# A GEGLU kernel on one core: the order of its first loads (gate rows on two queues ahead of the second block of x, the kept gate blocks in one stretch, then three transposing transfers)

## Chip, cores, metric

The kernel runs on one NeuronCore of one Trainium2 chip. The metric is the device time of one execution in microseconds (us), lower is better.

## The reference

```python
# x: 32 x 32 x 1024 (1024 tokens), w_gate, w_up: 1024 x 3584, w_down: 3584 x 1024, all bf16
def reference(x, w_gate, w_up, w_down):
    return (gelu(x @ w_gate) * (x @ w_up)) @ w_down      # tanh form of gelu
```

## The kernel before

The kernel multiplies by a one-level Strassen scheme: each matrix is cut into four quarters and some products are made on sums of quarters. TensorE (PE) runs almost without a pause. The first work it gets is a set of products "ahead": 24 column tiles of the lower rows of `w_gate` (the kept blocks `a12a` and `a12b`, numbers 0 to 5, four tiles each) times one quarter of the transposed x (`b21`). They need little data, so they fill the time in which the rest of x and the weights arrive.

The head, cut to what matters here (SyncE and ScalarE each issue to a DMA queue, q1 and q10 on the page; `KD` is 4 blocks of 128 rows, `KQ` is 2):

```python
load_nat(nc.sync, 0, 0, HALF)              # first block of x, not transposed: half on each queue
load_nat(nc.scalar, 0, HALF, NB_P)
...
load_ahead(0, 0, 1)                        # first gate rows, 128 KB, SyncE
load_nat(nc.scalar, 1, 0, NB_P)            # second block of x, 128 KB in packets of 256 B, ScalarE
load_ahead(0, 1, 2)                        # second gate rows, 128 KB, SyncE
load_xT(0, KD + KQ, DT)                    # transposing transfer, SyncE
load_ahead(1, 0, KQ, nc.scalar)            # 256 KB of gate rows, ScalarE
...                                        # all further loads are on SyncE
load_halves(2); load_halves(3)             # (each 2 x 256 KB)
for which in (1, 0): load_w_all(0, which)  # weights of the first chunk
load_halves(4)
load_xT(0, 0, KD)                          # b11, transposing, 512 KB
load_xT(1, 0, KD)                          # b12, transposing
load_ahead(5, 0, KD)
load_xT(1, KD, DT)                         # b22, transposing
for which in (1, 0): load_w_all(1, which)
```

What PE does with it, in program order:

```python
for _ in range(NWARM): matmul(warm_ps, ones, ones)     # 6 warm-up matmuls of 512 columns
transposed(0)                       # first block of x: 4 PE transposes, 2 VectorE copies into b21
# then, of the products ahead: row block 0 of group 0, first half of the columns (4 matmuls of 256)
transposed(1)                       # second block of x
# then the rest of groups 0 and 1 (36 more matmuls: 12 of 256 columns, 24 of 512), groups 2, 3, 4
tt(t1, b12, b11, SUB)               # VectorE: the first of the sums of x
...                                 # added, t2, t3, s3, t4, next chunk's s1: a long run on VectorE
group_ahead(5, ...)
# main loop over chunks: float32 products of sums, e.g. prod(psc[fl], s1[fl], t1, True)
```

In the profiles, `x_nat` is the untransposed x, `tp` the PE transposes, `a12a`/`a12b` the kept gate blocks, `b` a quarter of x, `t` the sums of x.

## Time and profile before

| | |
|---|---|
| time, median of the first 3 runs | 274.03 us (273.82 to 274.19) |
| PE busy | 266.5 of 272.0 us |
| first gate product starts | 4.70 us |
| second pair of transposes starts | 5.23 us |
| first VectorE sum of x starts | 21.62 us |

PE bounds the kernel: whatever does not move PE's start, or open a gap on it, is worth nothing. The timeline of the head of the kernel before (start, length, engine, line, operation, count, and in brackets the idle time before it and what ended it; PEld is the weight load):

```profile
3.29 0.63 PE L261 MATMUL tp<-ident,x_nat 128*128 128x128 bf16 x4
4.70 0.39 PE L281 MATMUL psC<-b,a12a 128*128 128x256 bf16 x2 [0.78 <-DMA a12a<-in_w_gate_dram]
4.92 0.38 PE L281 MATMUL psA<-b,a12a 128*128 128x256 bf16 x2
5.22 0.23 PEld L261 LDWEIGHTS <-x_nat 128*128 128x128 bf16 x4 [0.20 <-DMA x_nat<-in_x_dram]
5.23 0.40 PE L261 MATMUL tp<-ident,x_nat 128*128 128x128 bf16 x4
5.46 0.38 PE L281 MATMUL psC<-b,a12a 128*128 128x256 bf16 x2
```

PE waits 0.78 us for the first gate rows, makes four products, and then waits again, 0.20 us at the weight load, for the second block of x. Two matmuls of 256 columns take 0.38 us here. The times to landing of the transfers issued in the first 1.55 us (KB each, us from issue to landing):

```profile
a12a<-in_w_gate_dram SPq DMA_DIRECT2D x1, 128.0 KB, 3.4
x_nat<-in_x_dram ACTq DMA_DIRECT2D x1, 128.0 KB, 3.9
```

SyncE's queue and VectorE later on, kernel before, timeline:

```profile
11.07 6.55 SPq L215 DMA_TRANSPOSE b<-in_x_dram  x2
17.67 0.58 SPq L208 DMA_DIRECT2D a12b<-in_w_gate_dram  x1
18.30 4.29 SPq L215 DMA_TRANSPOSE b<-in_x_dram  x1
22.64 0.58 SPq L135 DMA_DIRECT2D wu<-in_w_up_dram  x1
...
21.62 2.29 DVE L342 TENSOR_TENSOR t<-b,b 128x2048 fp32r<-128x2048 bf16 x1 [1.87 <-DMA b<-in_x_dram]
```

Most plain issues take about half a microsecond; a transposing one holds SyncE's queue for up to 4.6 us (the two of the first line are 4.61 and 1.90). VectorE waits for the second transposing transfer before its first sum of x, and then runs without a pause to about 43 us. From 7 to 10 us, with SyncE's queue alone at work, the DMA moves 344 GB/s; the prediction reckons with about 330.

### The profile page before, as it was taken

How to read it: one execution, taken by the hardware profiler on the slowest of the kernel's cores; microseconds unless marked ns; L12 is line 12 of the kernel's file. 1: busy time of each engine (PE TensorE's matmuls, PEld its weight loads, DVE VectorE, ACT ScalarE, POOL GpSimd, SP SyncE). 2: the span in 40 equal slices, each digit the busy share in tenths (PEclk: the TensorE clock that was granted, in tenths of full speed). 3: DMA queues.
4: the chain of work that ended last, by engine and by line, in shares of the span. 5: the costliest groups of instructions: out<-in, count | busy, mean ns of one | idle time of the engine just before them, and what ended most of it. 6: DMA issues, size and time to landing. Idle time of an engine off the chain costs nothing.

```text
span 272.0 us, 3354 instructions
## 1 busy us (share of the span) xinstructions
PE 266.5 (98%) x1182; PEld 191.4 (70%) x1198; DVE 193.3 (71%) x204; ACT 112.9 (41%) x185; POOL 118.6 (44%) x60
## 2 busy tenths in 40 slices
PE   7999999999999999999999999999999999999995
PEld 4444777877877878778778776764447888888883
DVE  1448998786685676765855556459999999999511
ACT  2435765355454643654546436430300023972001
POOL 1090099989787796796786966000000000000000
PEclk9999999999999999999999999999999999999999
DMA  7999130540523504505225090005992435686202
GB/s 170 324 263 254 32 113 15 145 133 23 157 68 86 155 17 140 142 12 157 84 72 154 22 322 7 0 2 157 350 302 80 138 132 186 219 280 205 78 0 77
DMA packets 55888, 35.86 MB, mean 132 GB/s; under 512 B 9792, under 2 KB 55872, under 8 KB 55872
## 3 DMA queue, kind: packets, MB, share of 16 engines
q1 hardware_dynamic: 52496, 33.10, 42.5%
q10 hardware_dynamic: 3376, 2.56, 2.9%
q8 instruction: 9, 0.15, 0.2%
q14 instruction: 7, 0.06, 0.1%
HBM read 31.72 MB, written 2.10 MB: 124 GB/s over the span
## 4 chain that ended last, share of the span: by engine, by line
PE 97%; DMA 1%; issue 0%; ACT 0%; SPq 0%
PE psA L270 37%; PE psC L270 19%; PE psA L419 18%; PE psC L419 7%; PE psB L419 7%; PE psB L281 3%; PE psC L281 3%; PE psA L281 2%; DMA a12a<-in_w_gate_dram 1%; PE psB L270 1%; ACT o_sb L559 0%; SPq L197 0%; PE tp L261 0%
## 5 line engine op out<-in xcount | busy, mean ns | idle before, releaser
L270 PE MATMUL psA<-t,s 128*128 128x512 f32 x224 | 58.3, 402 | 0.0
L245 ACT ACTIVATE h<-c 128x512 bf16<-128x512 f32 x56 | 34.3, 629 | 39.3 <-DVE c L300 39.3
L270 PEld LDWEIGHTS psA<-t,s 128*128 128x128 f32 x224 | 42.1, 188 | 9.9
L170 POOL TENSOR_TENSOR s<-wu 128x1024 fp32r<-128x1024 bf16 x13 | 29.4, 2262 | 32.7 <-DMA wu<-in_w_up_dram 28.3
L171 POOL TENSOR_TENSOR s<-s,wg 128x1024 fp32r<-128x1024 f32 x14 | 30.1, 2147 | 14.8 <-PE psA L270 13.7
L173 POOL TENSOR_TENSOR s<-wg,wu 128x1024 fp32r<-128x1024 bf16 x13 | 28.9, 2223 | 0.0
L270 PE MATMUL psC<-t,s 128*128 128x512 f32 x112 | 27.9, 391 | 0.0
L270 PE MATMUL psA<-t,a22r 128*128 128x512 f32 x112 | 27.9, 391 | 0.0
L270 PE MATMUL psC<-b22r,s 128*128 128x512 f32 x112 | 27.7, 389 | 0.0
L270 PE MATMUL psA<-b,wg 128*128 128x512 bf16 x102 | 25.6, 380 | 0.4
L305 ACT COPY sn<-psC 128x512 f32<-128x512 f32 x28 | 16.3, 588 | 23.3 <-PE psC L270 15.9
L270 PEld LDWEIGHTS psC<-t,s 128*128 128x128 f32 x112 | 21.0, 188 | 4.5
L270 PEld LDWEIGHTS psA<-t,a22r 128*128 128x128 f32 x112 | 21.0, 188 | 4.4
L270 PEld LDWEIGHTS psC<-b22r,s 128*128 128x128 f32 x112 | 21.0, 188 | 4.4
L300 DVE TENSOR_TENSOR c<-sn,psC 128x512 f32<-128x512 f32 x28 | 19.1, 687 | 6.6 <-PE psC L270 6.6
L300 DVE TENSOR_TENSOR c<-sn,psA 128x512 f32<-128x512 f32 x28 | 19.1, 682 | 6.4 <-PE psA L270 6.4
L318 DVE TENSOR_TENSOR hi<-h,psA 128x512 bf16<-128x512 bf16 x14 | 9.6, 688 | 18.0 <-PE psA L270 18.0
L270 PEld LDWEIGHTS <-wg 128*128 128x128 bf16 x128 | 11.4, 98 | 15.5 <-issue 3.7
L172 POOL TENSOR_TENSOR s<-wg,s 128x1024 fp32r<-128x1024 bf16 x10 | 21.5, 2150 | 0.8
L305 ACT COPY sn<-psA 128x512 f32<-128x512 f32 x32 | 18.4, 590 | 7.2 <-PE psA L270 7.1
L300 DVE TENSOR_TENSOR c<-ahead,psA 128x512 f32<-128x512 f32 x24 | 16.3, 686 | 3.7 <-PE psA L270 2.5
L398 DVE TENSOR_TENSOR lo<-c,h 128x512 bf16<-128x512 f32 x14 | 17.9, 1275 | 0.5
(90 smaller groups left out, 381.0 us busy)
## 6 DMA issues: line engine op xcount, KB each, us to landing
wu<-in_w_up_dram SPq DMA_DIRECT2D x14, 512.0 KB, 3.9
wdb<-in_w_down_dram SPq DMA_DIRECT2D x12, 512.0 KB, 4.7
wg<-in_w_gate_dram SPq DMA_DIRECT2D x9, 512.0 KB, 5.1
wdb<-in_w_down_dram SPq DMA_DIRECT2D x12, 384.0 KB, 4.3
v<-in_w_down_dram SPq DMA_DIRECT2D x4, 512.0 KB, 6.4
out_dram<-o_sb ACTq DMA_DIRECT2D x16, 128.0 KB, 1.7
a12b<-in_w_gate_dram SPq DMA_DIRECT2D x6, 256.0 KB, 5.5
wg<-in_w_gate_dram SPq DMA_DIRECT2D x6, 256.0 KB, 4.6
```

The costliest lines, as they stand in the source:

```text
L170: yield engs[0].tensor_tensor(s1, a21, a22, ADD)
L171: yield engs[1].tensor_tensor(s2, s1, a11, SUB)
L172: yield engs[2].tensor_tensor(s4, a12, s2, SUB)
L173: yield engs[3].tensor_tensor(s3, a11, a21, SUB)
L245: nc.scalar.activation(h, src, ACT.Gelu_apprx_tanh)
L270: nc.tensor.matmul(ps, lhsT=lhs[:, k, :], rhs=rhs[:, k, :], start=(start and k == 0), stop=(k == KD - 1), skip_group_check=True,)
L281: nc.tensor.matmul(ps[:, cols], lhsT=a12_ahead[i][:, k, j * P : (j + 1) * P], rhs=b21[:, k, cols], start=(k == 0 and not cols.start), stop ...
L300: tt(t, s, ps, ADD)
L305: nc.scalar.copy(t, ps)
L318: tt(g_of(ft)[:, :NB], h0, psa, MUL)
L398: tt(g_of(ft)[:, NB:], added(sn5[fl], psa[fl]), h1[fl], MUL)
L419: nc.tensor.matmul(banks[m], lhsT=lhs(k)[:, m * P : (m + 1) * P], rhs=rhs(k), start=(start and k == 0), stop=(k == HF - 1), skip_group_che ...
```

## The change

The intent: PE should get its first gate rows sooner, by splitting them over both queues ahead of the second block of x; and the kept gate rows should come in one stretch, so that no plain load stands between the transposing ones.

```diff
-        load_ahead(0, 0, 1)
+        load_ahead(0, 0, 1, nc.sync, 0, KB // 2)        # 64 KB on SyncE
+        load_ahead(0, 0, 1, nc.scalar, KB // 2, KB)     # 64 KB on ScalarE
         load_nat(nc.scalar, 1, 0, NB_P)
 ...
         for which in (1, 0):
             load_w_all(0, which)
-        load_halves(4)
+        load_ahead(4, 0, KD)
+        load_ahead(5, 0, KD)
         load_xT(0, 0, KD)
         load_xT(1, 0, KD)
-        load_ahead(5, 0, KD)
         load_xT(1, KD, DT)
```

(`load_ahead` got two arguments for the columns; `load_halves` only moved up. The amount of work and of bytes is the same.)

More of the change, by code (lines that the diff above doesn't have):

```diff
@@ L204, with load_ahead, load_halves @@
         load_nat(nc.scalar, 0, HALF, NB_P)
-        def load_ahead(i, k0, k1, eng=nc.sync):
+        def load_ahead(i, k0, k1, eng=nc.sync, j0=0, j1=KB):
             f0 = i * KB
             eng.dma_start(
-                out=a12_ahead[i][:, k0:k1, :],
-                in_=wg_r[:, KD + k0 : KD + k1, f0 * P : (f0 + KB) * P],
-            )
+                out=a12_ahead[i][:, k0:k1, j0 * P : j1 * P],
+                in_=wg_r[:, KD + k0 : KD + k1, (f0 + j0) * P : (f0 + j1) * P],
+            )
+        def load_halves(i):
+            for k in range(0, KD, KQ):
+                load_ahead(i, k, k + KQ)
         def load_xT(nb, d0, d1):
@@ L226 @@
             load_ahead(i, KQ, KD)
-        def load_halves(i):
-            for k in range(0, KD, KQ):
-                load_ahead(i, k, k + KQ)
         load_halves(2)
```

## The prediction

> **What bounds the kernel now.** TensorE. The page shows PE busy 266.5 of 272.0 us (98%); the chain of waits is PE for 97%. The timeline shows PE without a gap from 5.23 us on; the wait view has only 0.8 us, before the first gate product. So the change can move the total only by moving PE's start in the first 6 us, or by opening a new gap on PE later.
>
> **The first 6 us (timeline, time to landing).** The first gate rows (128 KB) are issued at 1.24 us and land at 4.65; the first product starts at 4.70. Four products (about 0.11 us each) end near 5.14, and the next PE instructions, the second pair of transposes, wait 0.2 us at the weight load for the second block of x: issued at 1.25, landed about 5.13. They start at 5.23. PE takes these in order, so the second block of x is already as late as the gate rows: earlier gate rows alone are worth under 0.1 us.
>
> **What the change does here.** The gate rows become two 64 KB transfers, both issued near 1.24; the second block of x is issued one issue later (0.5 us, the measured spacing on that queue). [...] In the trace the second block's packets start near 3.1 us, about 1.85 after issue, and take about 1.1. Estimates from these:
> - gate rows land at 3.9 to 4.2, first product at about 4.15 (the eviction of the first transposes ends its first half at about 4.0): 0.5 us earlier;
> - second block of x lands at 5.4 to 5.6; second transposes start at about 5.55 instead of 5.23, PE idling about 0.9 us before them.
> Net on PE: about 0.3 us later.
>
> **The later reordering.** Before, the queue held gate block 4, two transposing transfers, block 5, one transposing transfer. Each transposing issue blocks SyncE [...] (4.61, 1.90, 4.29 us), so block 5 is issued at 17.67 and the DMA share falls near 19.4 to 20.3 and 22 to 22.6. After: blocks 4 and 5, then three transposing transfers, without these holes. Block 5 (512 KB at about 330 GB/s, 1.55 us) now precedes the first two, so the second lands at about 22.5 to 23 instead of 21.5; the third at about 23.7 instead of 24.7, the next weights some 1 us earlier. The first VectorE sum of x (starts 21.62 after waiting 1.87) starts up to 1.5 us later, and the busy DVE run behind it moves along. Slack on PE, from the timelines: sum t2 ends 27.3, used 29.5; next chunk's first weight sum ends 33.99, used 36.56; the second, on POOL, ends 36.27, used 38.38; accumulator banks released 42.2 and 42.9, used 43.8 and 44.7. All at least 1.6 us, so no PE gap. Off the critical path: 0 us, at worst 0.5.
>
> **Predicted:** 274.3 us (274.03 + 0.3), range 273.6 to 274.9. Faster by over 2%: 0.5%; within 2%: 99%; slower: 0.5%.
>
> **Right if** the first gate product starts about 0.5 us earlier, the PE wait moves to the second block of x, the next stretch of PE starts 0.2 to 0.4 later, and PE from 6 us on has no new gap although the DVE sum starts later.
>
> **Wrong if** the second block of x lands no later than now (gain up to 0.1), or the DVE run loses more than about 1.6 us (PE gaps near 36 to 44 us, up to 1 us).

## More of the kernel before

The page of the profile, its busy times, clock row and chain (the row of digits has 40 slices, each in tenths):

```profile
span 272.0 us, 3354 instructions
PE 266.5 (98%) x1182; PEld 191.4 (70%) x1198; DVE 193.3 (71%) x204; ACT 112.9 (41%) x185; POOL 118.6 (44%) x60
PEclk9999999999999999999999999999999999999999
...
PE 97%; DMA 1%; issue 0%; ACT 0%; SPq 0%
```

## The result, and the profile after

| | before | after |
|---|---|---|
| time, median | 273.92 us (273.42 to 274.50, 6 runs) | 274.29 us (273.73 to 274.52, 6 runs) |
| ratio | | 1.0011, 95% interval 0.9995 to 1.0027 |
| span of the profiled run | 272.0 | 272.7 |

A ratio is the mean time of one kernel's fast runs over that of the other's of the same rounds, so not quite the ratio of the medians quoted. The prediction was 274.3, range 273.6 to 274.9. So the number was hit; but the interval of the ratio includes 1, and the range would have been hit by a forecast of no change as well. Whether the reason was right is another question. The profile after, first the page:

```profile
span 272.7 us, 3354 instructions
PE 267.8 (98%) x1182; PEld 192.0 (70%) x1198; DVE 197.0 (72%) x204; ACT 112.5 (41%) x185; POOL 119.4 (44%) x60
PEclk9999999999999999999999999999999999999999
```

The timeline of its head:

```profile
4.09 0.58 PE L282 MATMUL psC<-b,a12a 128*128 128x256 bf16 x2 [0.17 <-DVE b L265]
4.47 0.63 PE L282 MATMUL psA<-b,a12a 128*128 128x256 bf16 x2
5.13 0.34 PEld L262 LDWEIGHTS <-x_nat 128*128 128x128 bf16 x4 [0.52 <-DMA x_nat<-in_x_dram]
5.14 0.61 PE L262 MATMUL tp<-ident,x_nat 128*128 128x128 bf16 x4
5.54 0.63 PE L282 MATMUL psC<-b,a12a 128*128 128x256 bf16 x2
5.96 0.64 PE L282 MATMUL psA<-b,a12a 128*128 128x256 bf16 x2
6.39 0.51 PE L282 MATMUL psC<-b,a12a 128*128 128x256 bf16 x2
6.74 0.38 PE L282 MATMUL psA<-b,a12a 128*128 128x256 bf16 x2
```

The first product starts 0.61 us earlier and the wait has moved to the second block of x, as predicted. But that block is not late: the second transposes start at 5.14, which is 0.09 before those of the kernel before. And yet PE was 0.62 us behind by 27 us (its first float32 product starts at 27.93, before at 27.31). The lines show where: two matmuls of 256 columns take 0.63 us until about 6.6 us and 0.38 only then. From the second transposes (5.14) to 6.65, PE ran at half rate for 1.5 us more, with matmuls of 256 columns 0.21 us apart instead of 0.11; before, it was at full rate by then. The trace's clock record has its first entry at 3.86 us before and at 6.65 us after. The page does not show this: its PEclk row reads 9 in both kernels, ahead of the first entry too.

SyncE's queue and VectorE after, timeline:

```profile
11.55 11.10 SPq L219 DMA_TRANSPOSE b<-in_x_dram  x3
22.70 0.58 SPq L135 DMA_DIRECT2D wu<-in_w_up_dram  x1
...
23.10 2.29 DVE L343 TENSOR_TENSOR t<-b,b 128x2048 fp32r<-128x2048 bf16 x1 [2.73 <-DMA b<-in_x_dram]
```

The three transposing issues hold the queue for 11.10 us in one piece; the next weights are issued at 22.70, not some 1 us earlier as predicted but when they were before (22.64). The first sum of x starts 1.48 us later, as predicted.

### The profile page after: what moved, and what is told of

It reads as the page before. It is cut to its first block, busy times and chain, and to the rows that moved or that the text cites. A ratio compares the mean times of both kernels' runs of the same rounds, so it can differ in the third digit from the quotient of the medians.

```text
span 272.7 us, 3354 instructions
## 1 busy us (share of the span) xinstructions
PE 267.8 (98%) x1182; PEld 192.0 (70%) x1198; DVE 197.0 (72%) x204; ACT 112.5 (41%) x185; POOL 119.4 (44%) x60
## 4 chain that ended last, share of the span: by engine, by line
PE 98%; issue 0%; ACT 0%; DVE 0%
PE psA L271 37%; PE psC L271 19%; PE psA L420 18%; PE psC L420 7%; PE psB L420 7%; PE psC L282 3%; PE psA L282 3%; PE psB L282 3%; PE psB L271 1%; PE psA L254 1%; PE tp L262 0%; ACT o_sb L560 0%; DVE b L265 0%
## 5 line engine op out<-in xcount | busy, mean ns | idle before, releaser
L399 DVE TENSOR_TENSOR lo<-c,h 128x512 bf16<-128x512 f32 x14 | 18.6, 1331 | 0.5
```

The costliest lines, as they stand in the source:

```text
L399: tt(g_of(ft)[:, NB:], added(sn5[fl], psa[fl]), h1[fl], MUL)
```

## The experiments

The theories:
- **On record**: the second block of x lands later and PE starts 0.3 us later.
- **C** (clock): PE's rate doubles (matmuls of 256 columns 0.21 us apart, then 0.11) at a moment that differs from execution to execution, whatever the kernel.
- **S**: the change itself makes the doubling come later, or costs time in some other systematic way.
- **D**: the later run on VectorE costs PE time.

### The two kernels again, and each half of the change alone

`before_again` and `after_again` have no edit. `split_only`:

```diff
-        load_ahead(4, 0, KD)               # against the changed kernel
-        load_ahead(5, 0, KD)
+        load_halves(4)
         load_xT(0, 0, KD)
         load_xT(1, 0, KD)
+        load_ahead(5, 0, KD)
```

`blocks_only`:

```diff
-        load_ahead(0, 0, 1, nc.sync, 0, KB // 2)      # against the changed kernel
-        load_ahead(0, 0, 1, nc.scalar, KB // 2, KB)
+        load_ahead(0, 0, 1)
```

before_again:

> The kernel before, unchanged, profiled a second time. In the first profile of before the matmuls of 256 columns start 0.11 us apart from 4.70 us on; in the profile of after they start 0.21 us apart until about 6.6 us and only then 0.11. Theory C (the doubling of TensorE's rate comes at a moment that differs from execution to execution, whatever the kernel): the moment in this profile differs from 4.1 us by up to 3 us either way, and the runs of this one kernel spread over about 1 us (273.4 to 274.5). Theory S (the change itself makes it come later): the doubling comes before 4.7 us again and the spread of the runs is under 0.4 us. Ratio to before 1.000 +- 0.002 under both.

after_again:

> The changed kernel, unchanged, profiled a second time. Theory C: its doubling differs from 6.9 us of the first profile, anywhere between about 3.5 and 7.5 us; if it comes before 5 us the span is about 0.1 us under that of the first profile of before (272.0). Theory S: doubling at 6.5 to 7 us again, span 272.5 to 272.8. Both: the second block of x lands at 5.0 to 5.2 us (the theory on record, 5.4 to 5.6, is contradicted by the first profile already).

split_only:

> Only the first part of the change: the gate rows split over both queues ahead of the second block of x; blocks 4 and 5 and the transposing transfers as before. Theory C: first gate product about 4.1 us, second transposes 5.1 to 5.2, first VectorE sum of x starts at about 21.6; time within 0.4 us of before in either direction. The prediction on record: second transposes at 5.55, time +0.3. Theory S with the cost in the split: +0.3, doubling late.

blocks_only:

> Only the second part: gate blocks 4 and 5 in one stretch, then three transposing transfers; head as before. All theories that call this free: second transposes near 5.23, the first VectorE sum of x at about 23.1 us, no PE gap after 6 us, time within 0.4 us of before. If the later VectorE run costs PE time (rival D): a PE gap between 30 and 46 us of 0.1 us or more, time up by as much.

Measured (all ratios against before in the same rounds, whose 11 runs had a median of 273.89, 273.37 to 274.53):

| run | median us (range) | ratio, 95% interval |
|---|---|---|
| before_again | 273.94 (273.89 to 274.11) | 1.0000, 0.9986 to 1.0015 |
| after_again | 274.61 (273.69 to 276.52) | 1.0027, 0.9997 to 1.0058 |
| split_only | 274.33 (274.31 to 274.67) | 1.0017, 1.0002 to 1.0032 |
| blocks_only | 274.11 (273.58 to 274.92) | 1.0008, 0.9991 to 1.0025 |

No run is 2% from before, and only one interval leaves out 1. The six profiles say more than the times. In the table each has one number per step; us from the span's start, "doubling" is the first entry of the clock record:

| profile | head | second block of x lands | second transposes | doubling | first float32 product | from there to the product with s3 of the second chunk (45.37 in before) |
|---|---|---|---|---|---|---|
| before | old | 5.15 | 5.23 | 3.86 | 27.31 | 18.06 |
| before_again | old | 4.55 | 4.97 | 5.37 | 27.23 | 18.04 |
| blocks_only | old | 4.65 | 4.71 | 3.77 | 27.38 | 18.08 |
| after | split | 5.08 | 5.14 | 6.65 | 27.93 | 18.12 |
| after_again | split | 5.38 | 5.43 | 5.09 | 27.50 | 18.79 |
| split_only | split | 5.38 | 5.40 | 5.52 | 27.68 | 18.08 |

Landings are the issue (1.25 us with the old head, 1.78 with the split) plus the time to landing, which the profile gives to a tenth.

**The doubling is not tied to the change.** The same code doubled at 3.86 and 5.37, and at 6.65 and 5.09. Theory S in its clock form (late again in after_again, early again in before_again) has fallen. The spread that C expected for before_again did not show (0.22 us in its five runs), but it did in before (1.16 us in the same rounds).

**The second block of x does land later with the split**, only not in the pair of profiles that happened to come first. The mean of three is 4.78 with the old head and 5.28 with the split, 0.5 later, just the one issue by which it was moved back; the second transposes start at 4.97 and 5.32 in the mean, 0.35 later. Three profiles a side are few, and the ranges overlap. Two later runs, sum_twice and one_warm, have the loads of the old head unchanged: their second block lands at 5.1 and 4.3, so the mean of five is about 4.75, and the half microsecond stays. The very first profile of before was a slow one: gate rows after 3.4 us and x after 3.9, against 2.9 and 3.3 in before_again:

```profile
a12a<-in_w_gate_dram SPq DMA_DIRECT2D x1, 128.0 KB, 2.9
x_nat<-in_x_dram ACTq DMA_DIRECT2D x1, 128.0 KB, 3.3
```

So the gain of 0.6 us on the first product, too, depends on the execution. In before_again the first product starts at 4.14, in blocks_only at 4.19, with the split at 4.09. But the first profile is not alone: in sum_twice the rows again took 3.4 us and the first product started at 4.68. The timeline of before_again, then of after_again:

```profile
4.14 0.61 PE L281 MATMUL psC<-b,a12a 128*128 128x256 bf16 x2 [0.23 <-DMA a12a<-in_w_gate_dram]
4.54 0.63 PE L281 MATMUL psA<-b,a12a 128*128 128x256 bf16 x2
4.97 0.58 PE L261 MATMUL tp<-ident,x_nat 128*128 128x128 bf16 x4
5.39 0.38 PE L281 MATMUL psC<-b,a12a 128*128 128x256 bf16 x2
```

```profile
4.09 0.58 PE L282 MATMUL psC<-b,a12a 128*128 128x256 bf16 x2 [0.17 <-DVE b L265]
4.47 0.63 PE L282 MATMUL psA<-b,a12a 128*128 128x256 bf16 x2
5.43 0.40 PE L262 MATMUL tp<-ident,x_nat 128*128 128x128 bf16 x4 [0.33 <-DMA x_nat<-in_x_dram]
5.66 0.38 PE L282 MATMUL psC<-b,a12a 128*128 128x256 bf16 x2
```

Here, with near equal doubling (5.37 and 5.09), one sees the trade that the split makes: 0.05 us won at the first product, 0.46 lost at the second transposes. The scatter of the landings is still in both numbers.

**The sum of the head closes.** Against the first profile of before, the first float32 product should be late by (a) the later start of the second transposes, (b) half of the time that PE still ran at half rate after that, (c) further waits for gate rows, read from the timeline (0.58 us in blocks_only before 8.57 us; 0.15 in split_only, where the starts of matmuls are 0.26 instead of 0.11 us apart near 7.1 us):

| | (a) | (b) | (c) | sum | measured |
|---|---|---|---|---|---|
| before_again | -0.26 | 0.20 | 0 | -0.06 | -0.08 |
| blocks_only | -0.52 | 0 | 0.58 | 0.06 | 0.07 |
| after | -0.09 | 0.75 | 0 | 0.66 | 0.62 |
| after_again | 0.20 | 0 | 0 | 0.20 | 0.19 |
| split_only | 0.17 | 0.06 | 0.15 | 0.38 | 0.37 |

The first pair of profiles differs by the clock (+0.75) with a small term the other way (-0.09); the split's own term (a) is 0.35 us between the means of the two heads. Since the terms are read from the same timelines, the table shows where the time of each profile went, not how often it goes there.

**Rival D is right for one execution.** In after_again the first sum of x started at 23.79, not 23.10, and PE lost another 0.75 us between 27 and 46 us (18.79 against 18.04). The largest piece is where a sum on VectorE still reads the accumulator bank that the next product goes into. VectorE and PE in after_again:

```profile
23.79 2.29 DVE L343 TENSOR_TENSOR t<-b,b 128x2048 fp32r<-128x2048 bf16 x1 [3.84 <-DMA b<-in_x_dram]
...
41.15 0.68 DVE L301 TENSOR_TENSOR c<-sn,psA 128x512 f32<-128x512 f32 x1
```

```profile
40.56 1.07 PE L271 MATMUL psA<-t,a22r 128*128 128x512 f32 x4
41.88 1.20 PE L271 MATMUL psA<-t,a22r 128*128 128x512 f32 x4 [0.25 <-DVE c L301]
```

The sum ends at 41.83, PE goes on at 41.88. In before the same sum ends at 39.66 and the same product starts at about 41.10 (40.19 plus four matmuls of 0.227), a slack of 1.44 us, and it is not in the prediction's list. By the starts, PE lost about 0.4 us at this point and 0.1 in the next few matmuls. Another 0.18 had gone just after 29.6, where the product with sum t2 starts: t2 ends at 29.48 here (27.3 in before). No wait is named there, so that piece is read from the starts only. In blocks_only (first sum at 22.89) and after (23.10) the slack was enough: 18.08 and 18.12.

### The same four with the clock held up: a failed design

The idea: hold the first loads back by about 8 us of VectorE work and warm PE up with 30 matmuls, so that the rate has doubled before the head starts.

```diff
-    NWARM = 6
+    NWARM = 30
 ...
+        nc.vector.memset(b21, 0.0)
+        for _ in range(3):
+            tt(t1, b21, b21, SUB)
+        nc.vector.memset(x_nat, 0.0)       # the loads of x_nat wait for this
         load_nat(nc.sync, 0, 0, HALF)
```

steady_before:

> The kernel before with the loads of the head held back by a fixed run of VectorE work (about 8 us) and 30 warm-up matmuls in place of 6, so that TensorE's rate has doubled before the first product in every execution. Result stays right. The base for its three sisters. Theory C: the spread of its runs falls from about 1 us to under 0.4 us; its time is some 8 us above before. From the landing of the first half block of x to the second transposes about 2.35 us, as in the first profile of before (2.87 to 5.23).

steady_after:

> The changed kernel with the same hold-back. Theory C (what separated the two profiles was the moment of doubling; at equal rate the change only moves the second transposes from 5.23 to 5.14): 0.05 to 0.15 us under steady_before. The prediction on record (second block of x later): 0.3 us above it. Theory S (something in the change costs time at full rate): 0.2 us or more above it.

steady_split:

> Only the split of the gate rows, with the hold-back. Theory C: 0.05 to 0.15 us under steady_before, same as steady_after. On record: +0.3.

steady_blocks:

> Only the reordering of blocks 4 and 5 and the transposing transfers, with the hold-back. On record and Theory C: 0 +- 0.05 us against steady_before. Rival D (the later VectorE run costs PE time): 0.05 us or more above it.

Measured medians: steady_before 283.96 (283.04 to 285.56), steady_after 284.73 (283.71 to 285.43), steady_split 284.32 (283.76 to 285.04), steady_blocks 284.10 (283.56 to 285.02), ratios to before 1.0356, 1.0380, 1.0370 and 1.0361. The spread did not shrink (2.5 us in steady_before, where under 0.4 was expected), and the base is 9.9 us above before and not 8, so nothing of 0.1 us can be read from them. The timeline of steady_before shows why:

```profile
11.59 0.39 PE L265 MATMUL tp<-ident,x_nat 128*128 128x128 bf16 x4 [1.68 <-DMA x_nat<-in_x_dram]
13.58 0.61 PE L285 MATMUL psC<-b,a12a 128*128 128x256 bf16 x2 [1.60 <-DMA a12a<-in_w_gate_dram]
```

The warm-up ended too soon, PE waited 1.68 and 1.60 us, and the rate fell again: the clock record has full rate from 5.76 to 12.58 and half rate to 19.41. In all four the half-rate stretch is 3.41 or 6.83 us long. The granted clock listed with every run tells the two cases apart: 0.994 in the profiled runs with 3.41 us at half rate, 0.988 in those with 6.83. Among the runs at 0.994 the medians are 283.92 (steady_before, 5 runs), 284.30 (steady_after, 3), 284.22 (steady_split, 5) and 283.74 (steady_blocks, 4). The two with the split are 0.3 to 0.4 above the base, as the record's step has it and against Theory C's 0.05 to 0.15 under it. But runs of one kernel still spread over 0.8 to 1.2 us, and this sorting was made after the fact: it is a hint, no evidence.

### The second block of x one place later still

```diff
-        load_nat(nc.scalar, 1, 0, NB_P)        # against split_only
         load_ahead(0, 1, 2)
         load_xT(0, KD + KQ, DT)
         load_ahead(1, 0, KQ, nc.scalar)
+        load_nat(nc.scalar, 1, 0, NB_P)
```

> As split_only, but the second block of x is issued one place later still, behind 256 KB of gate rows on its queue (issue at about 2.3 us instead of 1.78). The prediction on record made PE's start follow the landing of this block: issue 0.5 us later and 256 KB more ahead of it (about 0.8 us at 330 GB/s), so it lands at about 6.2 to 6.5 instead of 5.1 to 5.4, the second transposes start there, and the time is 0.7 to 1.1 us above split_only. If the time of the head is set by the moment of doubling alone (Theory C without the record's step), the time stays within 0.3 us of split_only.

Measured: 276.22 us (275.08 to 277.33), ratio 1.0070 (1.0032 to 1.0107); before in these rounds 274.10 (273.44 to 276.52). The six runs fall into two groups, 275.08 to 275.41 and 277.03 to 277.33. The block landed at about 6.65 (issue 2.27, 4.4 us to landing), and the timeline of the profiled run, one of the slower three, has

```profile
6.67 0.51 PE L262 MATMUL tp<-ident,x_nat 128*128 128x128 bf16 x4 [1.98 <-DMA x_nat<-in_x_dram]
6.97 0.64 PE L282 MATMUL psC<-b,a12a 128*128 128x256 bf16 x2
```

PE's start follows this landing, as the record said: the lower group is 0.8 us above split_only's median (of other rounds), as expected. The median of all six is 1.9 above it, outside the expected 0.7 to 1.1. The profiled run adds what was not expected: the clock record gives full rate from 3.40 to 6.81, half until 10.23, then full. The stretch at full rate holds the wait of 1.98 us, and the 3.42 us after it ran at half rate. By an estimate from these numbers that costs 1.7 us, half of 3.42; the two groups of times lie 1.9 apart. That the lower group kept its rate was not profiled, but its three runs list a granted clock of 1.000, where the profiled run with its 3.42 us at half rate lists 0.994. In the upper group two runs list 0.994, and the third, 277.03, lists 1.000: it lost its time in some other way. A late first doubling does not show in that number (one_warm, below, doubled at 9.25 and lists 1.000), but that it was one is not shown.

### The first VectorE sum twice

```diff
         tt(t1, b12, b11, SUB)
+        tt(t1, b12, b11, SUB)          # against before
```

> The kernel before, with the first VectorE sum of x done twice: the run of VectorE work behind it moves by 2.2 us, nothing else changes. The trace of before gives the tightest slack as 1.44 us: the sum that reads the second accumulator bank ends at 39.66 and the product that goes into this bank starts at about 41.1. So a PE gap of about 0.75 us (0.5 to 0.9) near 41 us, time +0.75 against before. It measures the slack that the reordering of the change eats into (its first sum started 1.5 us later in the first profile and 2.1 us later in the second, with a gap of 0.3 us named for VectorE). If the slack is 2.2 us or more: no gap, +0.

Measured: 275.09 us (274.90 to 275.84), ratio 1.0034 (1.0006 to 1.0062), the medians 0.99 apart. That is in keeping with a gap of 0.75, but the profile does not show one: it fell on an execution that doubled only at 8.84 us, so PE itself was 1.9 us late and the sum, though 2.3 us later, came in time (ends 41.95, needed at about 42.98). The slack of 1.44 is therefore shown by after_again, not by this run. What it does show is a late doubling with the unchanged head of before:

```profile
4.68 0.61 PE L281 MATMUL psC<-b,a12a 128*128 128x256 bf16 x2 [0.76 <-DMA a12a<-in_w_gate_dram]
5.08 0.63 PE L281 MATMUL psA<-b,a12a 128*128 128x256 bf16 x2
5.50 0.63 PE L261 MATMUL tp<-ident,x_nat 128*128 128x128 bf16 x4
...
7.64 0.63 PE L281 MATMUL psC<-b,a12a 128*128 128x256 bf16 x2
```

PE idled 0.76 us ahead of its first gate product here, and 0.23 in before_again, which doubled at 5.37. In before it idled 0.78 there, but had doubled at 3.86, ahead of that wait. Whether the wait made the doubling late is not shown.

### One warm-up matmul

```diff
-    NWARM = 6
+    NWARM = 1                          # against before
```

> The kernel before with one warm-up matmul in place of six. Theory C [...]: the busy stretch starts at about 4.1 us in place of 0.77, the doubling comes about 3.3 us later, at 7 to 10 us, matmuls of 256 columns are 0.21 us apart until then, and the time is 1.2 to 2.0 us above before, with a spread of at least 1 us. If the rate is not tied to the work before it: +0, within 0.3 us.

Measured: 275.71 us (275.18 to 276.67), ratio 1.0056 (1.0024 to 1.0088), the medians 1.6 apart; doubling at 9.25 us, with matmuls of 256 columns 0.21 us apart until then. The profile alone would not show the cause, since sum_twice doubled at 8.84 with six warm-ups. But all six runs took 275.18 or more, and the interval of the ratio leaves out 1: in this kernel the moment of the doubling hangs on the work before it. A doubling some 4 to 5.5 us later (9.25 against 3.77 to 5.37 in the first three profiles with six warm-ups and the old head) goes with 1.6 us. That is the size of the scatter that one profile can carry.

### The second gate rows behind the second block of x

The experiments pointed the other way from the change: get the second block of x in sooner, with fewer gate rows on the move beside it.

```diff
-        load_ahead(0, 1, 2)
+        load_ahead(0, 1, 2, nc.scalar)     # against before: now behind the second block of x
```

> The kernel before with its second gate rows (128 KB) moved from SyncE's queue to behind the second block of x on ScalarE's. A candidate that goes the other way from the change. If the second block of x lands late [...]: it lands at about 4.4 us in place of 4.55 to 5.13, second transposes at about 4.6 (rate doubled) or 4.95 (not yet), time 0 to 0.3 us under before. If its landing is set by its own packets: no change.

Measured: 276.17 us (275.22 to 278.18), ratio 1.0072 (1.0035 to 1.0109): a loss. The block did land at about 4.3 us (3.0 to landing; one_warm, with the order of before, had 4.3 too), and the second transposes followed the first products without a wait at 4.89. But then, in the timeline:

```profile
8.27 1.04 PE L281 MATMUL psA<-b,a12a 128*128 128x512 bf16 x4 [1.14 <-DMA a12a<-in_w_gate_dram]
```

With one issue less, SyncE's transposing transfer went out at 1.74 instead of 2.20, and the 256 KB of gate rows on ScalarE's queue went out at 2.34 instead of 1.78. These rows now took 5.9 us to land where before they took 4.5 and 3.9 in its two profiles, and PE waited 1.14 us for them. No run separates the two shifts, so which of them made the landing longer is not shown. The wait was moved, not removed. No version here beats the kernel before.

## Why the prediction was right, and where it was not

- **PE bounds the kernel and only the head counts**: right. In 13 of the 14 profiles PE takes 241.49 to 241.57 us from its first float32 product to its end; the other is after_again with 242.24.
- **"gate rows land at 3.9 to 4.2, first product at about 4.15 ... 0.5 us earlier"**: the landing and the start were right (about 4.1 and 4.09 in the three profiles with the split). The gain holds against a slow execution (4.70 in the first profile, 4.68 in sum_twice); against the other two of the table (4.14 and 4.19) it is 0.05 to 0.1.
- **"second block of x lands at 5.4 to 5.6; second transposes start at about 5.55 instead of 5.23"**: this is the step that was mis-sized. Measured 5.08 to 5.38, transposes at 5.14 to 5.43. The prediction shifted the packets of the block by 0.5 us and kept 1.1 us for their flow, from 3.1 us on. In the trace of before these packets run from 2.88 to 4.78, so 1.9 us. In the profile after they do start 0.7 us later (3.61), but they too end at 4.78. In these stretches both queues move packets side by side, 0.48 MB in before and 0.30 MB in after, of which the block is 0.13 each time: beside it 0.35 MB moved before and 0.17 after. That this is why it flowed faster is the author's estimate from these numbers; no run separates it. As a difference of means of three it holds, +0.35 against the +0.3 predicted, and moving the block one place further moved it again (6.67). The step is thus supported, though with three profiles a side whose ranges overlap (4.71 to 5.23 and 5.14 to 5.43). The pair of profiles that came with the result contradicts it: there the block landed no later than before, which is the prediction's own first "Wrong if".
- **The step that was missing**: PE's rate. The prediction took every matmul of 256 columns for 0.11 us because the one profile had doubled by 3.86 us. The moment lies anywhere from 3.4 to 6.65 with six warm-ups, or at 8.84 (sum_twice). It made 0.75 us in the first pair, whose total was 0.62; the landing made -0.09, and 0.04 is left over.
- **"All at least 1.6 us, so no PE gap ... 0 us, at worst 0.5"**: the list missed a bank with 1.44 us of slack. In three profiles with a shift of 0.9 to 1.5 us nothing was lost; in one with a shift of 2.2 us it was 0.75 us.
- **"the next weights some 1 us earlier"**: wrong; they were issued at 22.70 against 22.64, and at 23.60 in after_again. The third transposing transfer landed at 24.7 as before, not at 23.7. Three transposing issues in one piece held the queue to the same moment. It mattered for nothing.

In the first pair of profiles the right sum was luck: the clock made it, not the landing. Over all runs the sum came out right because a term of about +0.35, supported by the other profiles though not settled, was predicted as +0.3, and two unforeseen terms of up to 0.75 us are small enough for the range. What stays open: why the loads of the head land 0.5 us and more earlier in some executions than in others (gate rows of the old head: 3.8 to 4.65), what decides when the rate doubles, and how often the later VectorE run costs time (one of three profiles with the new block order).

## What to carry to other kernels

When a change moves less than the kernel's own scatter, one profile a side can show the right sum for the wrong reason: profile the same kernel again before reading a difference of half a microsecond, and write the difference as a sum of terms that has to close. Read PE's rate from the spacing of its matmuls in the first 10 us, not from the clock row. The two loads that feed PE one after the other were one wait here: bringing the first forward at the expense of the second gained nothing (first product at 4.09 against 4.14 to 4.70, second transposes 0.35 later in the mean).

## What the traces showed besides

- A wait of PE and a fall of its rate stood side by side twice. In x_block_last PE idled 2.25 us of the full-rate stretch from 3.40 to 6.81 (1.98 of it in one wait), and the next 3.42 us ran at half rate. In steady_before PE waited 1.68 us up to 11.59 and 1.60 up to 13.58, and the rate fell at 12.58.
- The moment of the first doubling scatters for one and the same code: 3.86 and 5.37 in before, 6.65 and 5.09 in the changed kernel, and 8.84 in sum_twice, whose head is that of before.
- The profile's clock reads as full ahead of its first record: in the profile after, the row reads 9 while the matmuls run at half rate up to 6.6 us. In rows_behind_x there is no clock record at all, though two matmuls of 256 columns take 0.63 us until 5.7 and 0.38 from 6.1 on.
- A transposing transfer held the issuing queue for 1.34 to 4.61 us in before and for 1.34 to 5.57 in after, where three in a row took 11.10 us, against about 0.5 us for most plain issues.
